# MoE 1 weights converted with an integer addition, a normalisation moved to ScalarE, and a second copy of values loaded by DMA

## The chip, the core and the metric

The kernel runs on one core of a Trainium2 chip. The metric is the device time in microseconds of one execution, the median of several. A core has TensorE (matrix products), VectorE, ScalarE and GpSimd (element-wise work), and SyncE, whose queue ("SP's queue" below) issues most DMAs here. Each engine works through its own instructions in order and waits on semaphores for the others.

## The reference

Three layers follow each other. Attention has 4 batches and 8 heads, 512 local and 32 global tokens, head size 64; a local token sees the 32 global ones and the local ones within 32 positions:

```python
s_ll = np.where(np.abs(pos[:, None] - pos[None, :]) <= 32, scale * q_l @ k_l.T, -1e9)
a_l = sm(np.concatenate([scale * q_l @ k_g.T, s_ll], axis=-1))
out_l = a_l @ np.concatenate([v_g, v_l], axis=2)
out_g = sm(scale * q_g @ k_all.T) @ v_all
```

Then MoE 1, a dense layer over all 2176 tokens (512 to 2048 to 512), whose two weight matrices are given in float64:

```python
h = x @ w_in
x = np.maximum(0.01 * h, h) @ w_out
```

Then MoE 2: each token goes to one of 8 experts, by the largest of its cosine products with the experts' embeddings, and its result is scaled by the gate:

```python
out[mask] = gate_w[mask, None] * (np.maximum(x[mask] @ w1[e], 0.0) @ w2[e])
```

## The kernel before

**Attention** works on 16 pairs of heads. A pair has four units (two row blocks of 128 times two heads). For unit `u`, `S(u)` computes two blocks of scores of 128x224 (192 local keys and 32 global ones), VectorE adds the mask and takes the maximum (L213), ScalarE takes the exponential with its sum (L218), VectorE the reciprocal of the sum (L222, L223). Then the two blocks are normalised, one on GpSimd and one on VectorE:

```python
        for i in range(2):
            eng = "pv"[i]
```

`TR(u)` transposes the probabilities two slots later, `AV(p)` multiplies them with the values four slots later. A window of 192 keys plus 32 global ones takes two products, and so the values lie in two arrangements: `ve`, in blocks of 128 rows shifted by 32, and `vb`, which holds the first 64 rows of each following block and the 32 global rows. `load_v(n)` fills `ve` by five DMAs and `vb` by two copies on ScalarE (L116, L117). Both have two buffers. `QK` transposes queries and keys, `GS`, `GT` and `GA` do the global tokens for every second pair.

**The conversion.** The weights of MoE 1 come as 64-bit words, in 32 pieces of 128x512. TensorE's products need them as a high and a low part whose sum is the float32 value. `conv_load(i)` loads piece i (two buffers, `raw`); `conv_abs(i)` takes on ScalarE the absolute value of the upper words (L357); `conv_bits(i)` puts the float32 word together on VectorE by five operations (L367, L368, L371, L374, L375); `conv_add(i)` adds the contribution of the low words on GpSimd (L384); `conv_split(i)` copies the high part on ScalarE (L390) and takes the difference on GpSimd (L391). One call of `conv()` does `conv_split(i - 1)`, `conv_bits(i)`, `conv_add(i)`, `conv_abs(i + 1)` and `conv_load(i + 2)`.

**The order.** TensorE's order is that of the program. On the other engines a planner with its own costs places the instructions, by priority, before the kernel runs. Slots 0 to 20 of attention run alone, with a `conv()` at every second one. Then steps of MoE 1 (`L1(i, f)`: 12 products into the hidden layer, then a copy on ScalarE (L691), the leaky maximum on VectorE (L692), a cast on ScalarE (L694) and a difference on VectorE (L695); `L2(i, f)`: 6 products out of it) alternate with attention slots, 0.65 slots per step, and each step for the first two row groups makes one call of `conv()` or more until the 32 pieces are done. Row groups 2 to 7 follow with the rest of attention. MoE 2 comes last and is not touched.

Of the kernel before, what the change touches and what calls it, by code (L numbers as in the profile page):

```python
# [8 lines left out]
F32 = mybir.dt.float32  # L9
F32R = mybir.dt.float32r  # L10
BF16 = mybir.dt.bfloat16
I32 = mybir.dt.int32
U32 = mybir.dt.uint32
I64 = mybir.dt.int64
AF = mybir.ActivationFunctionType
ALU = mybir.AluOpType
AX = mybir.AxisListType

P = 128
BIG = 3.0e38  # L20
NEG = -8.0e9
TINY = 1.125 * 2.0 ** -15
# [3 lines left out]
def kernel(  # L26
# [16 lines left out]
    nc = tc.nc  # L43
    B, H, SL, D = q_l.shape
    SG = q_g.shape[2]
    S_ = SL + SG
    NT, DM = out.shape
# [3 lines left out]
    NC = SL // P  # L51
# [12 lines left out]
    wide = w_in.dtype == I64  # L64
# [3 lines left out]
    sb = ctx.enter_context(tc.tile_pool(name="sb", bufs=1))  # L68
# [36 lines left out]
    def load_v(n):  # L105
        b, h0 = n // HP, 2 * (n % HP)
        hs = slice(h0, h0 + 2)
        ve, vb = ves[n % 2], vbs[n % 2]
        nc.sync.dma_start(ve[0:32, 0], v_g[b, hs].rearrange("h s d -> s h d"))
        nc.sync.dma_start(ve[32:P, 0], v_l[b, hs, 0:96].rearrange("h s d -> s h d"))  # L110
        for h in range(2):
            nc.sync.dma_start(
                ve[:, 1:NC, h, :], v_l[b, h0 + h, 96:96 + 3 * P].rearrange("(c p) d -> p c d", p=P)
            )
        nc.sync.dma_start(ve[0:32, NC], v_l[b, hs, 480:512].rearrange("h s d -> s h d"))
        nc.scalar.copy(vb[0:64], ve[0:64, 1:NC + 1])  # L116
        nc.scalar.copy(vb[64:96], ve[0:32, 0:1].to_broadcast([SG, NC, 2, D]))  # L117
        values[n] = ve, vb


# [6 lines left out]
        out=mask[:, :, 0:WIN], in_=mask[:, :, 0:WIN], pattern=[[0, 3], [1, WIN]],  # L127
# [3 lines left out]
        out=mask[:, :, 0:WIN], in_=mask[:, :, 0:WIN], pattern=[[0, 3], [-1, WIN]],  # L131
# [20 lines left out]
    def bank_of(name):  # L152
        return bank[name] if name in bank else "T"
# [39 lines left out]
    def S(u):  # L193
        n, c0, h = u // 4, 2 * ((u // 2) % 2), u % 2
        kT, _ = qkT[n]
        r = slice(D * h, D * h + D)
        sp = ps.tile([P, 2, WK], F32, tag=bank_of("sp"), name="sp")
        for i in range(2):
            c = c0 + i
            if n < NPAD:  # L200
                nc.tensor.matmul(sp[:, i, :], qz[:, h, c * P:(c + 1) * P], kT[:, c, :], start=True, stop=True)
            else:
                nc.tensor.matmul(  # L203
                    sp[:, i, :], qz[r, n % 2, c * P:(c + 1) * P], kT[r, c, :], start=True, stop=True,
                    tile_position=(D * h, 0),
                )
        pr = prs[u % NPR]
        nm = att.tile([P, 2], F32, tag="nm", bufs=4, name="nm")
        sm = att.tile([P, 2], F32, tag="sm", bufs=4, name="sm")
        for i in range(2):  # L210
            c = c0 + i
            m = 0 if c == 0 else (2 if c == NC - 1 else 1)
            nc.vector.tensor_tensor_reduce(  # L213
                out=pr[:, i, 0:WK], in0=sp[:, i, :], in1=mask[:, m, :], scale=-0.125, scalar=BIG,
                op0=ALU.add, op1=ALU.min, accum_out=nm[:, i:i + 1],
            )
        for i in range(2):
            nc.scalar.activation(  # L218
                out=pr[:, i, 0:WK], in_=pr[:, i, 0:WK], func=AF.Exp, bias=nm[:, i:i + 1], scale=-1.0,
                accum_out=sm[:, i:i + 1],  # L220
            )
        nc.vector.tensor_scalar(out=sm, in0=sm, scalar1=1e-9, scalar2=None, op0=ALU.add)  # L222
        nc.vector.reciprocal(out=sm, in_=sm)  # L223
        for i in range(2):
            eng = "pv"[i]
            if eng == "a":
                nc.scalar.activation(out=pr[:, i, 0:WK], in_=pr[:, i, 0:WK], func=AF.Copy, scale=sm[:, i:i + 1])
            else:
                (nc.gpsimd if eng == "p" else nc.vector).tensor_scalar(  # L229
                    out=pr[:, i, 0:WK], in0=pr[:, i, 0:WK], scalar1=sm[:, i:i + 1], scalar2=None, op0=ALU.mult  # L230
                )
        units[u] = pr
# [91 lines left out]
    NCV = 2 * KF  # L324
    raws, temps = {}, {}

    def conv_dst(i):
        f = i // 2
        if i % 2 == 0:
            fs = slice(f % KH * P, (f % KH + 1) * P)  # L330
            return wih[f // KH][:, :, fs], wil[f // KH][:, :, fs]
        return woh[f // KH][:, f % KH, :].unsqueeze(1), wol[f // KH][:, f % KH, :].unsqueeze(1)

    def conv_load(i):
        f = i // 2
        if i % 2 == 0:
            src = w_in[:, f * P:(f + 1) * P].rearrange("(k p) f -> p k f", p=P)
            shape = [P, KM, P]
        else:
            src = w_out[f * P:(f + 1) * P, :].unsqueeze(1)  # L340
            shape = [P, 1, DM]
        if wide:
            t = att.tile([P, 2 * DM], I32, tag="raw", bufs=2, name="raw")
            t = t.rearrange("p (k n) -> p k n", k=shape[1])
            nc.sync.dma_start(t, src.bitcast(I32))
            raws[i] = t.rearrange("p k (n t) -> p k n t", t=2)
        else:
            t = att.tile([P, DM], F32, tag="raw", bufs=2, name="raw")
            t = t.rearrange("p (k n) -> p k n", k=shape[1])
            nc.sync.dma_start(t, src)  # L350
            raws[i] = t

    def conv_abs(i):
        if wide and i in raws:
            t0 = sb.tile([P, DM], I32, tag="x2T", bufs=2, name="t0")
            t0 = temps[i] = t0.rearrange("p (k n) -> p k n", k=raws[i].shape[1])
            nc.scalar.activation(out=t0.bitcast(F32), in_=raws[i][:, :, :, 1].bitcast(F32), func=AF.Abs)  # L357

    def conv_bits(i):
        if not wide or i not in raws:  # L360
            return
        raw = raws.pop(i)
        low, top = raw[:, :, :, 0], raw[:, :, :, 1]
        t0 = temps[i]
        t2 = sb.tile([P, DM], I32, tag="x2", bufs=2, name="t2")
        t2 = t2.rearrange("p (k n) -> p k n", k=raw.shape[1])
        nc.vector.tensor_scalar(out=t0.bitcast(F32), in0=t0.bitcast(F32), scalar1=TINY, scalar2=None, op0=ALU.max)  # L367
        nc.vector.tensor_scalar(  # L368
            out=t0, in0=t0, scalar1=3, scalar2=0x3FFFFFF8, op0=ALU.logical_shift_left, op1=ALU.bitwise_and
        )  # L370
        nc.vector.scalar_tensor_tensor(  # L371
            out=t2, in0=top, scalar=-0x40000000, in1=t0, op0=ALU.bitwise_and, op1=ALU.bitwise_or
        )
        nc.vector.tensor_scalar(out=t0, in0=t2, scalar1=-0x800000, scalar2=None, op0=ALU.bitwise_and)  # L374
        nc.vector.scalar_tensor_tensor(  # L375
            out=t0.bitcast(F32), in0=low.bitcast(U32), scalar=2.0 ** -52, in1=t0.bitcast(F32),
            op0=ALU.mult, op1=ALU.mult,
        )
        temps[i] = t0, t2

    def conv_add(i):
        if 0 <= i < NCV and wide:
            t0, t2 = temps[i]
            nc.gpsimd.tensor_tensor(out=t2.bitcast(F32), in0=t2.bitcast(F32), in1=t0.bitcast(F32), op=ALU.add)  # L384

    def conv_split(i):
        if 0 <= i < NCV:
            hi, lo = conv_dst(i)
            src = temps.pop(i)[1].bitcast(F32) if wide else raws.pop(i)
            nc.scalar.copy(hi, src)  # L390
            nc.gpsimd.tensor_tensor(out=lo, in0=src, in1=hi.bitcast(F32), op=ALU.subtract)  # L391

# [2 lines left out]
    def conv():  # L395
        with tc.high_priority(offset=0):
            conv_()

    def conv_():
        i = cv[0]  # L400
        if i > NCV:
            return
        cv[0] += 1
        conv_split(i - 1)
        conv_bits(i)
        conv_add(i)
        conv_abs(i + 1)
        if i + 2 < NCV:
            conv_load(i + 2)

# [545 lines left out]
    for ve, vb in zip(ves, vbs):  # L956
        nc.vector.memset(ve[32:64, NC], 0.0)
        nc.vector.memset(vb[96:P], 0.0)
    load_v(0)
    load_qk(1)  # L960
    load_qk(2)
    load_v(1)
    for i in range(2):
        conv_load(i)
    conv_abs(0)

    NU = 4 * NHP
    LAG, AVL = 2, 4
# [88 lines left out]
    k = 0  # L1057
# [3 lines left out]
    while k < len(steps):  # L1061
        i, f = steps[k]
# [17 lines left out]
        while credit >= 0.5 and (hold or slot < bound):  # L1080
            if not hold:
                hold = att_parts(slot)
                slot += 1
                h = (len(hold) + 1) // 2
# [6 lines left out]
        n = (len(halves) + 1) // 2  # L1091
# [6 lines left out]
        if pend_r:  # L1098
            st, t = pend_r.pop(0)
# [125 lines left out]
```

## Time and profile before

| | |
|---|---|
| median of 3 runs | 965.67 us (965.29 to 968.04) |
| profiled execution, its time | 967.12 us |
| profiled execution, its span | 965.4 us |
| mean granted TensorE clock | 0.967 |
| TensorE products busy | 899.1 us, 93% of the span |
| VectorE busy | 696.4 us, 72% |
| ScalarE busy | 564.2 us, 58% |
| GpSimd busy | 280.2 us, 29% |

The span runs from the first to the last instruction of the core. The granted clock is that of TensorE: 1.00 is 2.4 GHz, 0.50 is 1.2 GHz, and a figure between is the mean of a stretch that has both. Busy shares over the whole span hide that stretches have different limits; they are read by stretch below. Products are pipelined, so TensorE's busy time is an upper bound of what it needs.

### The profile page before, as it was taken

The numbers are of one execution on the slowest core, as the hardware profiler recorded it, in microseconds if no ns is written. First come the engines' busy times: TensorE is split into PE (matmuls) and PEld (weight loads), VectorE is DVE, ScalarE is ACT, GpSimd is POOL, SyncE is SP. The second block draws the span as 40 slices with busy tenths as digits, with TensorE's granted clock in tenths as the row PEclk, the third lists the DMA queues.
The fourth block names the chain that finished last, engine by engine and source line by source line (L and its number), as shares of the span: only waits on it lengthen the run. The fifth ranks groups of instructions, "written<-read, shape, count | busy, mean of one in ns | idle before, by whom it ended". The sixth has DMA issues, their size and how long they took to land.

```text
span 965.4 us, 16184 instructions
## 1 busy us (share of the span) xinstructions
PE 899.1 (93%) x5578; PEld 747.9 (77%) x5578; DVE 696.4 (72%) x1722; ACT 564.2 (58%) x1206; POOL 280.2 (29%) x316
## 2 busy tenths in 40 slices
PE   7688877979999999999999999997799999999997
PEld 5565766768888888887888888986687888888885
DVE  7999999997554554544553534564988999999996
ACT  6777545465545554454452323256477888888885
POOL 4767656663121121121110100020223321222211
PEclk9987988989999999999999999999799999999999
DMA  6843333341011011010000000254613416919650
GB/s 163 186 121 110 111 108 102 91 132 24 23 39 43 23 38 42 1 39 20 2 12 13 12 12 12 60 170 186 51 48 119 134 44 221 359 33 381 210 201 25
DMA packets 92454, 89.82 MB, mean 93 GB/s; under 512 B 61191, under 2 KB 69511, under 8 KB 92370
## 3 DMA queue, kind: packets, MB, share of 16 engines
q1 hardware_dynamic: 88146, 77.99, 26.6%
q0 software_dynamic: 4224, 10.78, 4.0%
q8 instruction: 45, 0.74, 0.4%
q14 instruction: 39, 0.32, 0.1%
HBM read 137.14 MB, written 11.63 MB: 154 GB/s over the span
## 4 chain that ended last, share of the span: by engine, by line
PE 62%; issue 5%; DVE 5%; DMA 3%; ACT 1%; POOL 0%; SPq 0%; POOLq 0%; DVEq 0%
PE hps L684 16%; PE hp L910 9%; PE yp L938 8%; PE yp L706 6%; PE yp L708 5%; PE yp L707 5%; PE sp L203 3%; PE av L252 2%; PE pp L238 1%; PE tp L924 1%; DVE w2s L865 1%; DVE w1s L865 1%; DMA ids<-idl 1%; PE lp L514 1%; DMA out_dram<-yo,ids 1%
## 5 line engine op out<-in xcount | busy, mean ns | idle before, releaser
L692 DVE SCALAR_TENSOR_TENSOR gf<-gf 128x256 f32<-128x256 f32 (+1 forms) x144 | 62.9, 445 | 121.0 <-ACT gf L691 120.7
L910 PE MATMUL hp<-w1s,xgT 128*128 128x512 f32 x528 | 139.0, 413 | 0.0
L691 ACT COPY gf<-hps 128x256 f32<-128x256 f32 (+1 forms) x144 | 50.1, 359 | 145.8 <-PE hps L684 143.3
L938 PE MATMUL yp<-w2s,ht 128*128 128x512 f32 x528 | 130.8, 396 | 1.0 <-DVEq L1189 1.0
L938 PEld LDWEIGHTS yp<-w2s,ht 128*128 128x128 f32 x528 | 98.8, 188 | 25.7 <-DVEq L1189 1.4
L706 PE MATMUL yp<-woh,g 128*128 128x512 f32 x272 | 115.4, 424 | 1.8 <-ACT g L694 1.8
L910 PEld LDWEIGHTS hp<-w1s,xgT 128*128 128x128 f32 x528 | 100.0, 196 | 21.2
L708 PE MATMUL yp<-woh,g 128*128 128x512 f32 x272 | 108.9, 400 | 4.3 <-DVE g L695 4.3
L229 POOL TENSOR_SCALAR pr<-pr,sm 128x224 f32<-128x224 f32 x64 | 65.4, 1021 | 160.5 <-DVE sm L223 130.3
L707 PE MATMUL yp<-wol,g 128*128 128x512 f32 x272 | 108.3, 398 | 0.0
L694 ACT CAST g<-gf 128x256 fp32r<-128x256 f32 (+1 forms) x144 | 55.3, 394 | 71.5 <-DVE gf L692 71.5
L695 DVE TENSOR_TENSOR g<-gf,g 128x256 fp32r<-128x256 f32 (+1 forms) x144 | 66.2, 468 | 31.2 <-ACT g L694 25.9
L684 PE MATMUL hps<-xs,wih 128*128 128x256 f32 x448 | 77.6, 296 | 11.0 <-DVE nm L213 11.0
L684 PEld LDWEIGHTS hps<-xs,wih 128*128 128x128 f32 x448 | 66.8, 195 | 18.4 <-DVE nm L213 12.3
L684 PE MATMUL hps<-xl,wih 128*128 128x256 f32 x448 | 72.9, 285 | 0.0
L684 PE MATMUL hps<-xs,wil 128*128 128x256 f32 x448 | 72.6, 285 | 0.0
L946 POOL DMA_INDIRECT out_dram<-yo,ids x22 | 26.2, 1191 | 157.0 <-ACT yo L945 150.2
L218 ACT ACTIVATE pr<-pr,nm 128x224 f32<-128x224 f32 x128 | 60.8, 477 | 18.2 <-DVE nm L213 17.9
L708 PEld LDWEIGHTS yp<-woh,g 128*128 128x128 f32 x272 | 51.6, 190 | 19.3 <-DVE g L695 7.1
L684 PEld LDWEIGHTS hps<-xs,wil 128*128 128x128 f32 x448 | 62.6, 194 | 0.0
L684 PEld LDWEIGHTS hps<-xl,wih 128*128 128x128 f32 x448 | 62.6, 194 | 0.0
L706 PEld LDWEIGHTS yp<-woh,g 128*128 128x128 f32 x272 | 51.4, 189 | 14.0 <-issue 4.6
(267 smaller groups left out, 1933.7 us busy)
## 6 DMA issues: line engine op xcount, KB each, us to landing
w1a<-in_moe_w_dram SPq DMA_DIRECT2D x12, 2048.0 KB
w2a<-in_moe_w_dram SPq DMA_DIRECT2D x12, 2048.0 KB
w1b<-in_moe_w_dram SPq DMA_DIRECT2D x12, 2048.0 KB
w2b<-in_moe_w_dram SPq DMA_DIRECT2D x12, 2048.0 KB
raw<-in_moe_w_in_dram SPq DMA_DIRECT2D x16, 512.0 KB
raw<-in_moe_w_out_dram SPq DMA_DIRECT2D x16, 512.0 KB
x2d<-x SPq DMA_DIRECT2D x16, 256.5 KB
kn<-in_k_l_dram SPq DMA_DIRECT2D x32, 128.0 KB
```

The source lines that it names most:

```text
L218: nc.scalar.activation(out=pr[:, i, 0:WK], in_=pr[:, i, 0:WK], func=AF.Exp, bias=nm[:, i:i + 1], scale=-1.0, accum_out=sm[:, i:i + 1],)
L229: (nc.gpsimd if eng == "p" else nc.vector).tensor_scalar(out=pr[:, i, 0:WK], in0=pr[:, i, 0:WK], scalar1=sm[:, i:i + 1], scalar2=None, op0 ...
L684: nc.tensor.matmul(hps, ws[a][:, k], xs[c][k], start=(a + c + k == 0), stop=((a, c) == (1, 0) and k == KM - 1))
L691: nc.scalar.copy(gf, hps[:, cs])
L692: nc.vector.scalar_tensor_tensor(out=gf, in0=gf, scalar=0.01, in1=gf, op0=ALU.mult, op1=ALU.max)
L694: nc.scalar.copy(g[:, 0], gf)
L695: nc.vector.tensor_tensor(out=g[:, 1], in0=gf, in1=g[:, 0].bitcast(F32), op=ALU.subtract)
L706: nc.tensor.matmul(yp, g[:, 0], hi, start=(f == 0), stop=False)
L707: nc.tensor.matmul(yp, g[:, 0], lo, start=False, stop=False)
L708: nc.tensor.matmul(yp, g[:, 1], hi, start=False, stop=(f == KF - 1))
L910: nc.tensor.matmul(hp_, xT[:, a, k, :], w[:, c, k, :], start=(a + c + k == 0), stop=(c == 1 and k == KM - 1))
L938: nc.tensor.matmul(yp, ht[:, a, f, :], w[:, c, f, :], start=(j + a + c + f == 0), stop=(j == c == 1 and f == 3))
```

## The change

Three edits. First, `conv_round(i)` takes the place of `conv_abs(i)`: besides the absolute value it has ScalarE multiply the low words by 2^-29 and convert them to integers, into a second tile that takes the buffers (`x2`) in which the result lay before. `conv_bits(i)` then puts the truncated float32 word together in place, and a single addition of integers on VectorE adds the rounded low part, which replaces the masking L374, the product L375 and GpSimd's addition L384. The result now lies in the buffers tagged `x2T`. Second, the block that GpSimd normalised goes to ScalarE. Third, `vb` is no longer copied by ScalarE from `ve`, but loaded by five DMAs of its own; one more part of it is cleared at the start.

```diff
-        nc.scalar.copy(vb[0:64], ve[0:64, 1:NC + 1])
-        nc.scalar.copy(vb[64:96], ve[0:32, 0:1].to_broadcast([SG, NC, 2, D]))
+        for h in range(2):
+            part = v_l[b, h0 + h, 96:96 + 3 * P].rearrange("(c p) d -> p c d", p=P)
+            nc.sync.dma_start(vb[0:64, 0:NC - 1, h, :], part[0:64])
+            nc.sync.dma_start(vb[64:96, :, h, :], v_g[b, h0 + h].unsqueeze(1).to_broadcast([SG, NC, D]))
+        nc.sync.dma_start(vb[0:32, NC - 1], v_l[b, hs, 480:512].rearrange("h s d -> s h d"))
...
-            eng = "pv"[i]
+            eng = "av"[i]
...
-    def conv_abs(i):
+    def conv_round(i):
+
         if wide and i in raws:
-            t0 = sb.tile([P, DM], I32, tag="x2T", bufs=2, name="t0")
-            t0 = temps[i] = t0.rearrange("p (k n) -> p k n", k=raws[i].shape[1])
-            nc.scalar.activation(out=t0.bitcast(F32), in_=raws[i][:, :, :, 1].bitcast(F32), func=AF.Abs)
+            pair = []
+            for k in range(2):
+                t = sb.tile([P, DM], I32, tag=("x2T", "x2")[k], bufs=2, name=f"t{k}")
+                pair.append(t.rearrange("p (k n) -> p k n", k=raws[i].shape[1]))
+            temps[i] = pair
+            nc.scalar.activation(out=pair[0].bitcast(F32), in_=raws[i][:, :, :, 1].bitcast(F32), func=AF.Abs)
+            nc.scalar.activation(out=pair[1], in_=raws[i][:, :, :, 0].bitcast(U32), func=AF.Copy, scale=2.0 ** -29)
...
         nc.vector.scalar_tensor_tensor(
-            out=t2, in0=top, scalar=-0x40000000, in1=t0, op0=ALU.bitwise_and, op1=ALU.bitwise_or
+            out=t, in0=top, scalar=-0x40000000, in1=t, op0=ALU.bitwise_and, op1=ALU.bitwise_or
         )
-        nc.vector.tensor_scalar(out=t0, in0=t2, scalar1=-0x800000, scalar2=None, op0=ALU.bitwise_and)
-        nc.vector.scalar_tensor_tensor(
-            out=t0.bitcast(F32), in0=low.bitcast(U32), scalar=2.0 ** -52, in1=t0.bitcast(F32),
-            op0=ALU.mult, op1=ALU.mult,
-        )
-        temps[i] = t0, t2
-
-    def conv_add(i):
-        if 0 <= i < NCV and wide:
-            t0, t2 = temps[i]
-            nc.gpsimd.tensor_tensor(out=t2.bitcast(F32), in0=t2.bitcast(F32), in1=t0.bitcast(F32), op=ALU.add)
+        nc.vector.tensor_tensor(out=t, in0=t, in1=low, op=ALU.add)
+        temps[i] = t
...
         conv_split(i - 1)
         conv_bits(i)
-        conv_add(i)
-        conv_abs(i + 1)
+        conv_round(i + 1)
...
         nc.vector.memset(vb[96:P], 0.0)
+        nc.vector.memset(vb[32:64, NC - 1], 0.0)
```

## Rows read from the trace of the kernel before

**Rows 1.** Busy time of each engine by stretch, granted clock, DMA share, GB/s.

```profile
core 0: us, PE busy (x) PEld busy (x) DVE busy (x) ACT busy (x) POOL busy (x), PEclk, DMA share, GB/s
8.00:85.50 77.50, 63.44 (x492) 46.89 (x492) 72.09 (x252) 59.05 (x166) 48.48 (x56) 0.90 0.62 152
85.50:230.00 144.50, 119.58 (x792) 97.30 (x791) 141.14 (x302) 77.35 (x196) 90.90 (x77) 0.91 0.36 104
230.00:500.00 270.00, 267.61 (x1985) 227.16 (x1984) 136.23 (x568) 132.27 (x384) 49.04 (x70) 0.99 0.10 25
```

**Rows 2.** Groups of VectorE, 0 to 230 us: busy, mean ns, idle before.

```profile
L375 DVE SCALAR_TENSOR_TENSOR t<-raw,t 128x512 f32<-128x512 uint32 x32 | 29.1, 911 | 0.3
L371 DVE SCALAR_TENSOR_TENSOR t<-raw,t 128x512 int32<-128x512 int32 x32 | 26.7, 833 | 0.7
...
L367 DVE TENSOR_SCALAR t<-t 128x512 f32<-128x512 f32 x32 | 24.9, 778 | 0.9 <-ACT t L357 0.8
L374 DVE TENSOR_SCALAR t<-t 128x512 int32<-128x512 int32 x32 | 19.7, 614 | 0.0
L229 DVE TENSOR_SCALAR pr<-pr,sm 128x224 f32<-128x224 f32 x35 | 18.9, 541 | 0.1
L695 DVE TENSOR_TENSOR g<-gf,g 128x256 fp32r<-128x256 f32 x23 | 18.4, 800 | 0.5 <-ACT g L694 0.5
...
L692 DVE SCALAR_TENSOR_TENSOR gf<-gf 128x256 f32<-128x256 f32 x23 | 14.8, 645 | 0.0
```

**Rows 3.** Single lines, 0 to 230 us: count, then shortest, median, longest ns.

```profile
L371 DVE SCALAR_TENSOR_TENSOR t<-raw,t x32: 666/692/1786, 21.2 to 222.4; 128x512 int32<-128x512 int32 x32
...
L374 DVE TENSOR_SCALAR t<-t x32: 403/416/1515, 22.8 to 224.2; 128x512 int32<-128x512 int32 x32
```

**Rows 4.** Groups of VectorE, 230 to 500 us.

```profile
L695 DVE TENSOR_TENSOR g<-gf,g 128x256 fp32r<-128x256 f32 x60 | 25.3, 422 | 14.8 <-ACT g L694 14.2 <-PE yp L708 0.5
...
L229 DVE TENSOR_SCALAR pr<-pr,sm 128x224 f32<-128x224 f32 x29 | 10.0, 343 | 0.8
```

**Rows 5.** Timeline, 150 to 170 us: start us, duration us, instruction.

```profile
157.09 1.50 POOL L391 TENSOR_TENSOR wol<-t,woh 128x512 fp32r<-128x512 f32 x1
157.37 1.50 DVE L695 TENSOR_TENSOR g<-gf,g 128x256 fp32r<-128x256 f32 x1
```

**Rows 6.** Timeline, 435 to 452 us; in brackets the idle time before.

```profile
449.24 0.62 ACT L116 COPY vb<-ve 64x512 f32<-64x512 f32 x1 [6.51 <-issue]
...
451.07 0.50 PE L706 MATMUL yp<-woh,g 128*128 128x512 f32 x1 [1.80 <-ACT g L694]
```

**Rows 7.** Groups of VectorE, 8 to 85.5 us.

```profile
L374 DVE TENSOR_SCALAR t<-t 128x512 int32<-128x512 int32 x9 | 5.7, 631 | 0.0
```

**Rows 8.** Groups of GpSimd, 0 to 230 us.

```profile
L384 POOL TENSOR_TENSOR t<-t,t 128x512 f32<-128x512 f32 x32 | 44.7, 1396 | 23.2 <-DVE t L375 17.6 <-DVE sm L222 4.0 <-DVE gm L287 1.0
L229 POOL TENSOR_SCALAR pr<-pr,sm 128x224 f32<-128x224 f32 x35 | 38.9, 1112 | 30.9 <-DVE sm L223 27.1 <-DVE gm L284 1.6 <-PE kp L178 1.0
L391 POOL TENSOR_TENSOR wol<-t,woh 128x512 fp32r<-128x512 f32 x16 | 22.8, 1423 | 8.8 <-ACT woh L390 8.8
```

**Rows 9.** Groups of ScalarE, 0 to 230 us.

```profile
L218 ACT ACTIVATE pr<-pr,nm 128x224 f32<-128x224 f32 x72 | 34.3, 477 | 16.7 <-DVE nm L213 16.6
L357 ACT ACTIVATE t<-raw 128x512 f32<-128x512 f32 x32 | 21.7, 677 | 9.3 <-DMA raw<-in_moe_w_out_dram 5.4 <-DMA raw<-in_moe_w_in_dram 3.8
...
L694 ACT CAST g<-gf 128x256 fp32r<-128x256 f32 x23 | 9.4, 407 | 34.7 <-DVE gf L692 34.7
...
L117 ACT COPY vb<-ve 32x512 f32<-32x512 f32 x10 | 6.2, 617 | 1.1 <-DMA ve<-in_v_g_dram 0.6
```

**Rows 10.** Timeline, 0 to 30 us (SPq: DMA issues of SP's queue).

```profile
5.96 0.48 SPq L115 DMA_DIRECT2D ve<-in_v_l_dram  x1
...
8.09 0.62 ACT L116 COPY vb<-ve 64x512 f32<-64x512 f32 x1 [0.26 <-DMA ve<-in_v_l_dram]
...
14.32 0.43 SPq L345 DMA_DIRECT2D raw<-in_moe_w_in_dram  x1
```

**Rows 11.** Waits of SP's queue, whole run: total us, times, longest us.

```profile
SPq L112 <- PE av L252: 14.3, 6, 4.5
```

More of the change, by code (lines that the diff above doesn't have):

```diff
@@ L362, in conv_bits @@
         raw = raws.pop(i)
[L363 to L367, printed above, removed]
+        top = raw[:, :, :, 1]
+        t, low = temps[i]
+        nc.vector.tensor_scalar(out=t.bitcast(F32), in0=t.bitcast(F32), scalar1=TINY, scalar2=None, op0=ALU.max)
         nc.vector.tensor_scalar(
-            out=t0, in0=t0, scalar1=3, scalar2=0x3FFFFFF8, op0=ALU.logical_shift_left, op1=ALU.bitwise_and
+            out=t, in0=t, scalar1=3, scalar2=0x3FFFFFF8, op0=ALU.logical_shift_left, op1=ALU.bitwise_and
         )
         nc.vector.scalar_tensor_tensor(
-            out=t2, in0=top, scalar=-0x40000000, in1=t0, op0=ALU.bitwise_and, op1=ALU.bitwise_or
+            out=t, in0=top, scalar=-0x40000000, in1=t, op0=ALU.bitwise_and, op1=ALU.bitwise_or
         )
-        nc.vector.tensor_scalar(out=t0, in0=t2, scalar1=-0x800000, scalar2=None, op0=ALU.bitwise_and)
-        nc.vector.scalar_tensor_tensor(
-            out=t0.bitcast(F32), in0=low.bitcast(U32), scalar=2.0 ** -52, in1=t0.bitcast(F32),
-            op0=ALU.mult, op1=ALU.mult,
-        )
-        temps[i] = t0, t2
-    def conv_add(i):
-        if 0 <= i < NCV and wide:
-            t0, t2 = temps[i]
-            nc.gpsimd.tensor_tensor(out=t2.bitcast(F32), in0=t2.bitcast(F32), in1=t0.bitcast(F32), op=ALU.add)
+        nc.vector.tensor_tensor(out=t, in0=t, in1=low, op=ALU.add)
+        temps[i] = t
     def conv_split(i):
@@ L388, in conv_split @@
             hi, lo = conv_dst(i)
-            src = temps.pop(i)[1].bitcast(F32) if wide else raws.pop(i)
+            src = temps.pop(i).bitcast(F32) if wide else raws.pop(i)
             nc.scalar.copy(hi, src)
@@ L964 @@
         conv_load(i)
-    conv_abs(0)
+    conv_round(0)
     NU = 4 * NHP
```

## The prediction

> **What bounds the kernel now.** I read the profile in four steps. First the busy time by stretch [rows 1]. The kernel has an attention part (slots 0 to 20, 8 to 85.5 us), a mixed part where MoE 1 steps and attention slots alternate and the weight conversion runs (85.5 to 230 us), and a part where the conversion is over (from 230 us). In the mixed part VectorE is busy 141.14 of 144.50 us, 98%, TensorE 119.58 and ScalarE 77.35. In the attention part VectorE has 72.09 of 77.50 us (93%), TensorE 63.44, ScalarE 59.05. From 230 to 500 us TensorE has 267.61 of 270.00 and VectorE half. So VectorE sets the pace up to 230 us and TensorE behind it, and the order of TensorE's work is fixed in the program: time won before 230 us moves everything behind it forward.
>
> Second, what VectorE does there [rows 2]. The five operations of a conversion piece, 32 pieces, lead the list (one, L368, is not shown). Their means are odd: 614 ns for L374, whose median is 416 [rows 3]; 833 for L371, median 692; 800 and 645 for the MoE 1 lines L695 and L692, where L695 takes 422 after 230 us [rows 4]. L367 reads one tensor and writes one, of L374's size, so I take 416 for its unhindered price too, against a mean of 778.
>
> Third, why. The timeline shows it [rows 5]: GpSimd's subtraction begins at 157.09 and takes 1.50 us; VectorE's L695 begins at 157.37 and also takes 1.50, and so ends with it or just behind. VectorE is stretched by GpSimd's work.
>
> The stretch, (mean − unhindered) × count, from rows 2 to 4: L375 (911−692)×32 = 7.0 us; L371 (833−692)×32 = 4.5; L367 (778−416)×32 = 11.6; L374 (614−416)×32 = 6.3; L229 (541−343)×35 = 6.9; L695 (800−422)×23 = 8.7; L692 (645−422)×23 = 5.1. In all 50 us, 44 without L374.
>
> Fourth, behind 230 us: one place where ScalarE, in order, sat 6.51 us before the copy L116 into the second set of values; TensorE then stood 1.80 us [rows 6].
>
> **The change part by part.**
>
> *VectorE, conversion.* L374 goes: 19.7 us [rows 2], of which 5.7 in the attention part [rows 7] and 14.0 in the mixed one. L375 becomes an integer addition of two tensors, 128x512. The trace has no such addition. Bounds: 416 ns (one source, as L374 in [rows 3]) and 911 (L375 as it is now); the nearest row is L371, two sources of the same size, 692 unhindered. I take 692, so it is worth nothing against L375 beyond the stretch below. The ends move VectorE by ∓9 us over both parts.
>
> *GpSimd, and the stretch.* In the first 230 us the four kinds that read large tiles take 44.7 (L384) + 38.9 (L229) + 22.8 and about as much again (the two halves of L391; one is shown) = 129 us [rows 8]. The change removes L384 and GpSimd's L229; 45 remain, 35%. If the stretch falls in proportion, 0.65 × 44 = 28.4 us go: conversion 15.0, L229 4.5, L692 and L695 9.0. Ten of the 32 pieces and 20 of the 35 halves lie in the attention part, which gets 7.3; the mixed part gets 21.1. The ends are 0 and 44.
> The Trainium skill ("SBUF — State Buffer", section "Who interferes with whom") states that GpSimd and VectorE share a port pair by an exclusive lock, held for a whole instruction, that the loser blocks fully, and that a VectorE operation with two SBUF inputs contends with a GpSimd operation that reads. Rows 5 agree: 1.50 us beside 1.50. That rule speaks against my proportion, since what counts is whether a subtraction is still there to block one operation, and this is a rival below.
>
> *ScalarE.* The conversion gains a pass per piece, over the low words. No row has ScalarE reading an integer; bounds are 407 ns (L694, half the elements) and 1.4 us (GpSimd's price for that size), nearest the Abs pass L357 with the same strided source, 677 [rows 8, 9]. I take 677: 10 × 0.677 = 6.8 us in the attention part, 22 × 0.677 = 14.9 in the mixed one. At 1.4 us it would cost the attention part 7 us and the mixed one nothing. One normalisation per unit comes from GpSimd, 128x224 between SBUF tiles: between L694's 407 and L218's 477 ns, so 0.44: 20 × 0.44 = 8.8 and 15 × 0.44 = 6.6 us. The two copies of 617 ns per load of values go [rows 9] (one of the two is shown): five loads in each part, 6.2 us each.
>
> *Sums by part.* Attention: VectorE 72.1 − 5.7 − 7.3 = 59.1; ScalarE 59.05 + 6.8 + 8.8 − 6.2 = 68.5; TensorE at most 63.4. The busiest is now ScalarE. Mixed: VectorE 141.1 − 14.0 − 21.1 = 106.0; ScalarE 77.35 + 14.9 + 6.6 − 6.2 = 92.7. TensorE has 119.6 at a mean granted clock of 0.91 [rows 1]. Between the two levels, 1.2 and 2.4 GHz, that is 18% of 144.5 us, 26 us, at the lower one, which can have cost 13 us. So TensorE needs 107 to 120 us; I take 113, as the lower clock follows its waits and about half of those should go.
>
> *How full.* The busiest engine filled 93% and 98% of these parts. ScalarE at 93% makes the attention part 73.7 us, 3.8 less. In the mixed part TensorE and VectorE are now near each other and wait for each other in turn; I take 92%: 113 / 0.92 = 122.8 us, 21.7 less.
>
> *Queues.* Each load of values has five more DMAs on SP's queue. SP issues one in about 0.48 us at the start, one right behind the other, and the first weights are issued at 14.32 [rows 10]. Two loads of values lie ahead of them: 2 × 5 × 0.48 = 4.8 us later at most, 0 if the queue's order puts the new ones behind. I count 1 us, in the attention part. The second copy itself comes 2.4 us of issue later, then lands like the last old DMA, which was issued at 5.96 and used at 8.09; in place of 1.2 us of copies. That is covered: values are first used four slots, some 15 us, after their pair begins. The added memset of 32x128 at the start is one small operation per buffer before VectorE is busy.
>
> *Behind 230 us.* The copy that held ScalarE [rows 6] is gone, so the 1.8 us and a little clock: I count 2 us, between 0 and 5 (2.4 us in which TensorE idled and 1% of clock, both in [rows 1], at half speed 2.7). The 29 normalisations that ScalarE gets there, 13 us, lie beside TensorE at 99% and ScalarE at 132 of 270. MoE 2 is untouched.
>
> Sum: 3.8 − 1 + 21.7 + 2 = 26.5 us. The profiled execution has a span of 965.4 us and a time of 967.12; the median of the three timed runs is 965.67. The gain is taken from the median: 939 us.
>
> **The rivals.**
> *ScalarE waits in order.* The Abs of piece i+1 now writes the buffer that the GpSimd subtraction of piece i−1 still reads, and that subtraction starts only after ScalarE's own copy in the same call. If Abs is queued right behind that copy, ScalarE sits about one subtraction, 1.4 us [rows 8], per piece, and behind it stand the exponentials and the copies that TensorE waits for. Attention: 68.5 + 14 = 82.5, 5 more than before; mixed: 92.7 + 30.8 = 123.5, at 98% 126, 18.5 less; with 2 behind, 950. It speaks against it that other ScalarE work can be put between. From 0.9 us per piece the attention part gets longer than it was.
> *Whole blocks.* Every remaining subtraction still catches one operation, since it and the four conversion operations come from one call: no stretch is saved. Mixed: VectorE 141.1 − 14.0 = 127, at 95% 134, 10.6 less; attention 3; behind 2: 950. By the lock rule of the Trainium skill (“SBUF — State Buffer”, “Who interferes with whom”), taken strictly, it would go this way.
> *Full clock.* With VectorE out of the way TensorE stays at the upper level: mixed 107 / 0.97 = 110, attention 68.5 / 0.97 = 70.6: 34 + 7 + 2 = 43 less, 922. The clock of 0.99 behind 230 us speaks for it, the mixed part's chains through three engines against.
> *Slower: the weights starve.* Ten loads of values before 230 us put 2.4 us of issue and a wait for the buffer's last reader, up to 4.5 us [rows 11], ahead of weight loads in SP's queue; ScalarE already waits for weights, 9.3 us in all at L357 [rows 9]. All of it exposed is 69 us. It decides from 38%: at half, 939 + 34.5 = 973. Against it: the old loads carry the same waits, and weight buffers come free two operations earlier.
>
> **How the numbers follow.** Forecast 0.58; ScalarE's waits 0.12; whole blocks 0.08; full clock 0.11; starved weights 0.07; gain and queue cancelling within 0.3%, about what a measurement of this kernel can tell from no change, 0.04. So faster 0.89, same 0.04, slower 0.07. The forecast's own range, from the ends of the clock (107 to 120 us), of the addition and of the stretch, is 929 to 948; with the rivals on the fast side, 920 to 956.
>
> **What would show it.** Right: between 8 us and the end of the conversion VectorE's share falls from 96% to some 85% and TensorE's rises; L367, L371, L692 and L695 near 0.42 to 0.7 us; conversion over near 204 us, and from there the old pace; ScalarE near full in the attention part; no wait of ScalarE for values at some 425 us. Wrong: ScalarE waiting for GpSimd before Abs, or for weights; means of L695 still near 0.8; an addition or a low-word pass of over 1 us; a mixed part above 135 us.

## The result and the profile after

The change makes the kernel 0.9% faster: 958.65 us median of four runs against 965.91, ratio 0.9914 with an interval of 0.989 to 0.9938. 939 was forecast, 26.5 us less; it came to 7.3 us less, outside the range of 920 to 956. Two of the three stretches came out near the forecast, the third 21 us worse.

The marks are the first product of MoE 1 and the first product of its 27th step (twelve products into the hidden layer make a step; from there on the steps follow at the same pace in all versions until attention goes on). Busy time by stretch, changed kernel, columns as in [rows 1], the marks at 103.3 and 233.6 us:

```profile
8.00:103.30 95.30, 72.68 (x492) 53.99 (x492) 77.04 (x264) 73.73 (x200) 24.17 (x34) 0.77 0.65 168
103.30:233.60 130.30, 120.23 (x839) 100.51 (x838) 97.60 (x265) 86.02 (x221) 31.47 (x32) 0.95 0.35 97
233.60:500.00 266.40, 265.94 (x1999) 225.90 (x1998) 139.54 (x578) 139.65 (x407) 22.73 (x41) 1.00 0.12 30
```

The kernel before, from its first MoE 1 product to its 27th step (the attention part stands in [rows 1]):

```profile
85.50:237.60 152.10, 127.18 (x839) 104.08 (x838) 143.77 (x309) 80.08 (x203) 91.78 (x78) 0.92 0.34 99
```

The attention part took 95.3 us in place of 77.5, 17.8 more. The mixed part took 130.3 in place of 152.1, 21.8 less. From the 27th step to the end of the span it is 724.3 in place of 727.8, 3.5 less. Together 7.5 us. In the attention part no engine is near full. The granted clock fell from 0.90 to 0.77 there, and TensorE's 492 products of the part were busy 72.68 us in place of 63.44. How much of the 17.8 us the lower clock made by itself, and how much it only followed from TensorE's waits, no run separates.

VectorE's groups, changed kernel, 0 to 230 us (beside [rows 2]; L377, L374, L373, L232, L688, L691 are the old L371, L368, L367, L229, L692, L695, and L380 is the integer addition):

```profile
L377 DVE SCALAR_TENSOR_TENSOR t<-raw,t 128x512 int32<-128x512 int32 x32 | 25.8, 805 | 0.5
...
L380 DVE CUSTOM_DVE_ANT_0 t<-t,t 128x1024 uint16<-128x1024 uint16 x32 | 24.2, 755 | 0.2
L374 DVE TENSOR_SCALAR t<-t 128x512 int32<-128x512 int32 x32 | 20.0, 624 | 0.4
L373 DVE TENSOR_SCALAR t<-t 128x512 f32<-128x512 f32 x32 | 17.6, 549 | 7.6 <-ACT t L364 7.3
L232 DVE TENSOR_SCALAR pr<-pr,sm 128x224 f32<-128x224 f32 x36 | 17.3, 482 | 0.8
L688 DVE SCALAR_TENSOR_TENSOR gf<-gf 128x256 f32<-128x256 f32 x25 | 12.7, 507 | 17.8 <-ACT gf L687 17.8
L691 DVE TENSOR_TENSOR g<-gf,g 128x256 fp32r<-128x256 f32 x24 | 10.9, 455 | 2.2 <-ACT g L690 2.2
```

L691 has come from 800 to 455 ns and L688 from 645 to 507: GpSimd's stretch is mostly gone there. In the conversion it is not: L377 has 805 ns where it had 833, and L374 has 624 where its counterpart L368, not shown in [rows 2], had 545:

```profile
L368 DVE TENSOR_SCALAR t<-t 128x512 int32<-128x512 int32 x32 | 17.4, 545 | 0.2
```

The mean of the addition holds stretch too. Its shortest, median and longest ns, 0 to 230 us:

```profile
L380 DVE CUSTOM_DVE_ANT_0 t<-t,t x32: 669/690/1781, 30.6 to 183.7; 128x1024 uint16<-128x1024 uint16 x32
```

ScalarE's groups in the attention part of the changed kernel:

```profile
L365 ACT ACTIVATE t<-raw 128x512 int32<-128x512 uint32 x15 | 10.1, 671 | 3.5 <-DMA raw<-in_moe_w_in_dram 2.5 <-DMA raw<-in_moe_w_out_dram 1.0
L364 ACT ACTIVATE t<-raw 128x512 f32<-128x512 f32 x15 | 10.0, 669 | 7.6 <-DMA raw<-in_moe_w_out_dram 4.1 <-DMA raw<-in_moe_w_in_dram 3.1 <-POOL wil L388 0.3
L230 ACT ACTIVATE pr<-pr,sm 128x224 f32<-128x224 f32 x20 | 9.5, 484 | 0.1
...
L387 ACT CAST wih<-t 128x512 fp32r<-128x512 f32 x7 | 4.3, 621 | 0.3 <-DVE t L380 0.3
L387 ACT CAST woh<-t 128x512 fp32r<-128x512 f32 x7 | 4.3, 610 | 2.1 <-DVE t L380 2.1
```

and of the kernel before, 8 to 85.5 us, the line that answers to L387:

```profile
L390 ACT CAST wih<-t 128x512 fp32r<-128x512 f32 x4 | 2.5, 624 | 0.0
L390 ACT CAST woh<-t 128x512 fp32r<-128x512 f32 x4 | 2.5, 616 | 0.0
```

Fourteen conversion pieces have their high part before the first MoE 1 product, where eight had: on ScalarE six pieces of the mixed part now go ahead of attention work. The timeline of ScalarE shows what that does:

```profile
48.99 0.66 ACT L364 ACTIVATE t<-raw 128x512 f32<-128x512 f32 x1 [2.75 <-DMA raw<-in_moe_w_in_dram]
49.55 0.66 ACT L365 ACTIVATE t<-raw 128x512 int32<-128x512 uint32 x1
...
51.52 0.67 ACT L365 ACTIVATE t<-raw 128x512 int32<-128x512 uint32 x1
...
52.84 0.68 ACT L364 ACTIVATE t<-raw 128x512 f32<-128x512 f32 x1
...
54.33 0.49 ACT L230 ACTIVATE pr<-pr,sm 128x224 f32<-128x224 f32 x1
```

and that of TensorE, behind it:

```profile
54.87 1.11 PE L241 MATMUL pp<-ident,pr 128*128 128x128 f32 x4 [6.41 <-ACT pr L230]
```

ScalarE sat 2.75 us for a weight load, then did four weight passes and other work, and only then the normalisation for which TensorE had stood 6.41 us. The four transposes that follow take 1.11 us; early in the part, at 19.78 to 25.69 us, four of them took 0.66. SP's queue shows why the weights were late:

```profile
6.49 0.74 SPq L118 DMA_DIRECT2D vb<-in_v_l_dram  x1
7.28 0.59 SPq L119 DMA_DIRECT2D vb<-in_v_g_dram  x1
...
22.14 0.43 SPq L348 DMA_DIRECT2D raw<-in_moe_w_in_dram  x1
```

The first weights are issued at 22.14 us in place of 14.32 [rows 10], 7.8 us later, where 4.8 was my upper bound: the ten added DMAs hold the queue for 6.2 us, most of them 0.6 us each and not 0.48, and other loads went ahead too.

### The profile page after: what moved, and what is told of

Its sections match the earlier page's. It is cut to its first block, busy times and chain, and to the rows that moved or that the text cites. A ratio compares the mean times of both kernels' runs of the same rounds, so it can differ in the third digit from the quotient of the medians.

```text
span 957.9 us, 16074 instructions
## 1 busy us (share of the span) xinstructions
PE 900.4 (94%) x5578; PEld 750.6 (78%) x5578; DVE 656.5 (69%) x1692; ACT 591.0 (62%) x1270; POOL 169.2 (18%) x220
## 4 chain that ended last, share of the span: by engine, by line
PE 72%; DVE 9%; DMA 7%; issue 6%; ACT 4%; SPq 2%; POOL 1%; POOLq 0%; DVEq 0%; ACTq 0%
PE hps L680 19%; PE hp L906 9%; PE yp L934 8%; PE yp L702 7%; PE yp L704 6%; PE yp L703 6%; PE sp L206 4%; DMA raw<-in_moe_w_in_dram 3%; PE av L255 2%; PE pp L241 2%; PE tp L920 1%; DMA raw<-in_moe_w_out_dram 1%; DVE w2s L861 1%; DVE w1s L861 1%; DMA ids<-idl 1%
## 5 line engine op out<-in xcount | busy, mean ns | idle before, releaser
L688 DVE SCALAR_TENSOR_TENSOR gf<-gf 128x256 f32<-128x256 f32 (+1 forms) x144 | 59.9, 424 | 129.0 <-ACT gf L687 128.7
L691 DVE TENSOR_TENSOR g<-gf,g 128x256 fp32r<-128x256 f32 (+1 forms) x144 | 58.4, 414 | 32.6 <-ACT g L690 28.0
L861 DVE TENSOR_TENSOR w2s<-w2a,w2s 128x1024 fp32r<-128x1024 f32 x48 | 56.7, 1218 | 2.8 <-ACT w2s L860 2.6
L861 DVE TENSOR_TENSOR w1s<-w1a,w1s 128x1024 fp32r<-128x1024 f32 x48 | 56.6, 1218 | 1.7 <-ACT w1s L860 1.6
## 6 DMA issues: line engine op xcount, KB each, us to landing
kn<-in_k_l_dram SPq DMA_DIRECT2D x32, 128.0 KB
```

Of the source, the lines that this page charges most:

```text
L688: nc.vector.scalar_tensor_tensor(out=gf, in0=gf, scalar=0.01, in1=gf, op0=ALU.mult, op1=ALU.max)
L691: nc.vector.tensor_tensor(out=g[:, 1], in0=gf, in1=g[:, 0].bitcast(F32), op=ALU.subtract)
L861: nc.vector.tensor_tensor(out=w[:, 1, c], in0=src[:, c], in1=w[:, 0, c].bitcast(F32), op=ALU.subtract)
```

## The experiments

The edits: 1 is the conversion, 2 the normalisation on ScalarE, 3 the second values by DMA. There are four theories. **Q**: the added DMAs put off the weights in SP's queue. **S**: in the attention part each us of ScalarE's work shows, full or not. **P**, against S: only the normalisation's place in the chain of a unit costs. **T**, beyond S: VectorE's work counts as well. The versions were timed beside the kernel before, whose medians were 966.5 to 967.2 us.

| | edits | median, us | ratio, interval | first MoE 1 product | 27th step | pieces by the first product |
|---|---|---|---|---|---|---|
| before | none | 965.91 | | 85.5 | 237.6 | 8 |
| changed | 1, 2, 3 | 958.65 | 0.9914 (0.989 to 0.9938) | 103.3 | 233.6 | 14 |
| e1 | 2 | 970.79 | 1.0035 (1.0017 to 1.0054) | 94.8 | 241.7 | 11 |
| e2 | 3 | 970.38 | 1.0016 (0.9995 to 1.0038) | 87.5 | 244.7 | 8 |
| e3 | 1 | 949.94 | 0.9807 (0.9771 to 0.9843) | 87.2 | 221.2 | 11 |
| e4 | 1, 2 | 953.39 | 0.9848 (0.9806 to 0.9889) | 96.7 | 225.3 | 13 |
| e7 | 1, 3 | 943.88 | 0.9773 (0.9733 to 0.9813) | 83.3 | 217.1 | 9 |
| e9 | 2, 3 | 964.77 | 0.9972 (0.9946 to 0.9998) | 90.6 | 240.5 | 8 |

The first product and the 27th step are in us, read from the one profiled execution of each version. The last column counts the conversion pieces whose high part is made (`conv_split`) by the first product.

**Each edit alone, and the change without the third.**

> The kernel before with the second edit alone: GpSimd's normalisation goes to ScalarE. Theory Q (SP's queue: the five added DMAs per load of values put off the weight loads, and ScalarE, in order, waits for the weights): this run has no added DMAs, so the first MoE 1 product stays near 85.5 us (103.3 us in the changed kernel) and the mixed part gains from less GpSimd work, 950 to 960 us. Theory S (ScalarE has too much work in the attention part): 8.8 us more on ScalarE there, first MoE 1 product at 88 to 92 us, 958 to 968 us.

> The kernel before with the third edit alone: the second copy of values by DMA. Theory Q: weights 5 to 8 us later at the start and again at each load, first MoE 1 product at 90 to 103 us, 966 to 980 us. Theory S: ScalarE is relieved of two copies per load, first MoE 1 product at 83 to 86 us, 958 to 966 us.

> The kernel before with the first edit alone: the conversion by the low words on ScalarE and an integer addition. Theory Q: first MoE 1 product at 82 to 87 us, mixed part some 15 us shorter, 942 to 952 us. Theory S: 6.8 us more on ScalarE in the attention part with the copies kept, first MoE 1 product at 88 to 95 us, 950 to 960 us.

> The changed kernel without its third edit: values copied by ScalarE again. ScalarE has then the most work of all versions in the attention part. Theory Q: first MoE 1 product at 82 to 90 us, 935 to 948 us. Theory S: first MoE 1 product at 103 us or later, 958 to 970 us.

The edits are the three parts of the diff of the change, taken singly (e1 `"pv"` to `"av"`; e2 the loads of `vb` and its memset; e3 the conversion), and e4 is e1 with e3. The conversion alone is worth 17 us, more than the whole change. The normalisation alone puts the first MoE 1 product 9.3 us later, in the direction that S said but beyond its 88 to 92 us, and with the conversion again 9.5 (e3 to e4). The DMAs alone put it 2.0 us later, less than Q had it; the time is in Q's range. From e4 to the changed kernel they cost 6.6 us in the attention part and 5.3 in time. The attention parts of e2, e3 and e4, as busy time by stretch with the columns of [rows 1]:

```profile
8.00:87.50 79.50, 66.85 (x491) 50.20 (x492) 69.71 (x242) 51.16 (x150) 47.86 (x55) 0.85 0.64 162
8.00:87.20 79.20, 61.87 (x490) 46.88 (x491) 68.30 (x248) 65.90 (x178) 38.62 (x49) 0.94 0.67 168
8.00:96.70 88.70, 70.86 (x491) 52.14 (x492) 78.04 (x261) 78.70 (x210) 24.52 (x33) 0.83 0.65 162
```

These three speak against S as it stands. In e2 ScalarE has 7.9 us less work than before and the part is no shorter; its first weights are issued late, at 23.67 us, which can have taken the gain. In e3 it has 6.9 us more, with 3.8 less on VectorE, and the part is 1.7 us longer. e4 has the most work on ScalarE of all versions, but its part is 6.6 us shorter than the changed kernel's. S missed both its marks in all four runs, in e3 narrowly; Q missed both in e1 and e4 and has the time alone in e2 and e3. So neither holds throughout.

**A spare pass of ScalarE.** It reads a constant, and nobody reads what it writes. Each run has the first line and one of the others:

```diff
+        spare = att.tile([P, WK], mybir.dt.uint8, tag="spare", bufs=1, name="spare")
+        nc.scalar.activation(out=spare, in_=mask[:, 0, :], func=AF.Copy, scale=0.5)      # e5
+        nc.scalar.activation(out=spare, in_=mask[:, 0, :], func=AF.Copy, scale=nm[:, 0:1])  # e10, e13
+        nc.vector.tensor_scalar(out=spare, in0=mask[:, 0, :], scalar1=nm[:, 0:1], scalar2=None, op0=ALU.mult)  # e14
```

> The kernel before with one more pass of ScalarE per unit, 128x224, that reads a constant and whose result nobody reads: the second edit's work on ScalarE without its place in the chain of a unit. Moving the normalisation alone put the first MoE 1 product from 85.5 to 94.8 us. Theory S (ScalarE has too much work): the spare pass does the same, 92 to 95 us. Theory P (the probabilities of a unit now stand in ScalarE's queue behind other work, where GpSimd was free at once): 85 to 89 us. Time by S 968 to 976, by P 964 to 970 us.

> As the spare pass before, but scaled by the unit's own maximum, so that it can't run ahead of its unit: one pass of 0.39 us on ScalarE per unit that nobody waits for (the earlier one ran ahead, 43 passes and 16.5 us before 100 us). Theory S: first MoE 1 product 8 us later than 85.5, at 92 to 96 us, 969 to 974 us. Theory P (the place in the chain of a unit costs, not the work): 85 to 88 us, 965 to 968 us.

e5 took 986.02 us (1.0182, 1.014 to 1.0224), first product at 104.2: the passes were bound to nothing and 43 of them, 16.5 us, ran between 8 and 100 us. e10 took 974.07 (1.007, 1.0048 to 1.0092), first product at 94.3. The spare passes of e10 (number, then least, median and longest ns, first and last start in us):

```profile
L223 ACT ACTIVATE spare<-mask,nm x64: 464/467/486, 11.0 to 492.3; 128x224 uint8<-128x224 bf16 x64
```

and its attention part, as busy time by stretch:

```profile
8.00:94.30 86.30, 67.90 (x492) 50.72 (x492) 80.94 (x254) 66.72 (x185) 52.01 (x58) 0.86 0.61 148
```

Twenty passes of 0.467 us, 9.3 us, put the first product 8.8 us later, as much as the normalisation did in e1, though nothing needs what they write and ScalarE is busy 77%. So the place in the chain is not all that costs, against P, and added work on ScalarE shows, as S says. VectorE is busy 80.94 us here, 94% of the part and 8.9 us more than before, so this run alone does not tell ScalarE's queue from a slowed VectorE. Over both parts it is less: some 36 passes, 16.8 us, put the 27th step 8.1 us later, half a us per us.

**The same pass on the version with edits 1 and 3, on either engine.**

> First and third edits (943.9 us, first MoE 1 product at 83.3 us) and a spare pass of 0.47 us on ScalarE per unit, as in the paced run. Theory S (ScalarE alone sets the pace of the attention part) and theory T (ScalarE and VectorE take turns, and the work of both counts): first MoE 1 product 7 to 10 us later, at 90 to 94 us; 947 to 952 us. If ScalarE, busy 56.5 of 75.3 us here, has room: 83 to 86 us and 943 to 946 us.

> The same spare pass on VectorE, some 0.2 to 0.4 us per unit, 4 to 8 us in the attention part, where VectorE is busy 63.4 of 75.3 us. Theory S: first MoE 1 product stays at 83 to 85 us, 943 to 946 us. Theory T: it comes later by about the added work, 88 to 92 us, 946 to 952 us.

On ScalarE, 952.45 us (0.9839, 0.98 to 0.9879): 8.6 us more than e7, first product at 98.7, beyond the 90 to 94 expected, 27th step 9.6 later. On VectorE, at 0.33 us a pass (median; 0.41 in the mean over both parts), 947.42 (0.9797, 0.9762 to 0.9832): 3.5 more, first product at 87.9, 27th step 3.6 later. The attention part of e7 (busy time by stretch, columns as in [rows 1], here and below):

```profile
8.00:83.30 75.30, 61.75 (x491) 47.37 (x491) 63.43 (x236) 56.50 (x161) 38.29 (x48) 0.95 0.68 173
```

Of e13:

```profile
8.00:98.70 90.70, 67.89 (x491) 51.12 (x492) 74.71 (x257) 70.59 (x194) 41.30 (x52) 0.84 0.66 166
```

Of e14:

```profile
8.00:87.90 79.90, 65.51 (x491) 50.29 (x492) 71.52 (x267) 58.62 (x164) 38.34 (x50) 0.84 0.71 174
```

By this VectorE's work would cost a quarter of a us per us over both parts, but the intervals of e7 and e14 overlap, so T is not shown. In e13 ScalarE has 14 us more, of which 9.9 are the spare passes: twelve pieces lie before the first product, where e7 has nine. So conversion pieces also go ahead of attention when ScalarE has more work, and the mixed part, 128.0 us against 133.8, gives some of it back.

How much of the delay is added work, and how much is pieces that went ahead? It can be read earlier, where nearly as many pieces are done on either side: at the first exponential of the 14th unit, in the kernel before, e10, e7, e13 and e14:

```profile
53.31 0.50 ACT L218 ACTIVATE pr<-pr,nm 128x224 f32<-128x224 f32 x1
59.85 0.48 ACT L218 ACTIVATE pr<-pr,nm 128x224 f32<-128x224 f32 x1
58.64 0.48 ACT L221 ACTIVATE pr<-pr,nm 128x224 f32<-128x224 f32 x1
64.92 0.50 ACT L221 ACTIVATE pr<-pr,nm 128x224 f32<-128x224 f32 x1
56.74 0.51 ACT L221 ACTIVATE pr<-pr,nm 128x224 f32<-128x224 f32 x1
```

and busy time by stretch up to there, in the kernel before, e10 and e13:

```profile
8.00:53.30 45.30, 35.79 (x292) 27.11 (x292) 41.36 (x154) 35.66 (x104) 27.20 (x33) 1.00 0.74 176
8.00:59.90 51.90, 41.36 (x305) 31.33 (x307) 47.25 (x157) 41.88 (x121) 28.38 (x34) 0.93 0.67 153
8.00:64.90 56.90, 42.02 (x305) 32.79 (x307) 42.28 (x160) 42.61 (x121) 22.16 (x31) 0.85 0.69 165
```

In e10 the unit comes 6.5 us later, behind 13 spare passes of 6.1 us in all, with four high parts made and five pieces begun on VectorE on either side. At the 8th and the 11th unit it is the same: 3.1 and 4.7 us later, behind 3.3 and 4.7 us of passes, with as many pieces done. So in e10 the added work shows whole without pieces going ahead; but VectorE is 91% busy in both, and its work, 157 instructions against 154, took 5.9 us longer. In e13, where VectorE is busy 74%, the unit comes 6.3 us later than in e7, behind 13 passes of 6.2 us, with five high parts in both and three weight passes (2 us) more. Here single units scatter: 0.7 us at the 8th, 8.8 at the 11th. In e14, with 14 passes on VectorE ahead of it, the unit comes 1.9 us earlier than in e7. Up to this point, then, added work on ScalarE shows nearly whole and added work on VectorE does not. Of the 15.4 us by which e13 is late at the first product, 9.1 come behind the 14th unit, with eight more passes (3.7 us) and three pieces that went ahead.

**Both halves on VectorE, and the changed kernel without its second edit.**

> The first edit, and both halves normalised on VectorE; values copied by ScalarE. VectorE gets 0.34 us more per unit, 7 us in the attention part, to 75 of 79 us, and meets less GpSimd work. Theory P: VectorE comes to the half some 0.4 us after the other, so the first MoE 1 product stays near the 87 us of the first edit alone, and the mixed part is shorter as GpSimd stretches VectorE less: 943 to 949 us. Theory S says the same of ScalarE. If VectorE becomes the bound of the attention part, first MoE 1 product at 90 us or later, 949 to 956 us.

> The changed kernel without its second edit: GpSimd normalises again. Theory P: without the normalisation in ScalarE's queue first MoE 1 product at 88 to 94 us and 950 to 955 us. Theory Q (the added DMAs put off the weights): the late weights alone cost 6 us or more against the first edit alone (949.9 us), so 956 us or more.

e6 (`"vv"` on e3) took 953.65 us (0.988, 0.9835 to 0.9926), first product at 97.4, 27th step at 223.7: taking the normalisation from GpSimd costs the attention part the same 10 us on VectorE as on ScalarE. Neither P nor S foresaw that; the third forecast, VectorE as the bound, did. VectorE is busy 90% of the part:

```profile
8.00:97.40 89.40, 66.74 (x492) 50.78 (x492) 80.40 (x280) 70.65 (x187) 24.70 (x33) 0.84 0.64 161
```

So what the second edit costs is not a matter of ScalarE alone.

e7 was better than either theory had it, 943.88. From e7 to the changed kernel the second edit alone costs 14.8 us.

**The first weights ahead.**

```diff
+    for i in range(2):
+        conv_load(i)
     load_v(0)
     load_qk(1)
     load_qk(2)
     load_v(1)
-    for i in range(2):
-        conv_load(i)
```

> The changed kernel with the first two weight loads ahead of the first loads of values in SP's queue. Theory Q, first loads: what the DMAs added to the attention part (first MoE 1 product at 103.3 us, against 96.7 without them) is the first weights' place, 22.1 us for their issue: they now go before 12 us, first MoE 1 product at 96 to 99 us, 951 to 955 us. Theory Q, all loads: later weights are put off as before, at most 2 us won, 956 to 960 us.

> The first and third edits, GpSimd normalising as before, and the first two weight loads ahead of the first values in SP's queue. With ScalarE normalising, the place of the first weights was worth 6.6 us. Theory Q: it is worth as much here, 936 to 940 us against 943.9. Theory S: with less work on ScalarE late weights hide, 942 to 945 us.

On the changed kernel (e8), 952.08 us (0.9849, 0.9814 to 0.9885), 6.6 less, first product at 92.3, its part with a clock of 0.88:

```profile
8.00:92.30 84.30, 66.45 (x490) 48.99 (x491) 70.39 (x252) 69.36 (x190) 22.75 (x32) 0.88 0.70 170
```

Without the second edit (e11), 943.56 (0.9748, 0.9714 to 0.9782), the same as e7, though its first product is at 87.2; in e7 the first weights are issued at 24.23 us, later still than in the changed kernel. Of these four versions, late first weights cost only where ScalarE normalises too: Q holds with S, not alone.

**Edits 2 and 3 without the conversion.**

> The second and third edits on the kernel before, the conversion left as it was. Added up from each alone (+3.4 and +3.2 us against the runs beside them): about 973 us. Theory S (each us of work on ScalarE in the attention part shows): the copies that go pay for most of the normalisation that comes, first MoE 1 product at 88 to 92 us, 967 to 972 us. Theory Q (the weights that are issued late stop ScalarE in order, and the normalisation behind it): first MoE 1 product at 97 us or later, 974 us or more.

964.77 us, less than either alone; the first product, 90.6, is in the range of S, by which the copies that go pay for the normalisation; but neither the sum, nor Q, nor S foresaw that the time would be below that of the kernel before.

**The second values issued from GpSimd's queue** (`nc.gpsimd` in place of `nc.sync` for `vb`, with edit 1).

> The first and third edits with the second copy of values issued from GpSimd's queue, GpSimd normalising. Theory Q: SP's queue is as short as before the change, first weights issued near 14 us, 936 to 942 us. If writing the descriptors on GpSimd holds up its normalisation and subtraction, or VectorE, first MoE 1 product at 90 us or later and 946 to 955 us.

964.24 us (0.9968, 0.9953 to 0.9983), beyond both forecasts, first product at 105.3 with 14 pieces ahead of it, though the first weights were issued at 13.2 us. GpSimd's issues, 0 to 230 us:

```profile
L118 POOL DMA_DIRECT2D vb<-in_v_l_dram x20 | 13.3, 667 | 7.2 <-PE av L255 7.0 <-issue 0.2
L119 POOL DMA_DIRECT2D vb<-in_v_g_dram x20 | 11.6, 589 | 0.0
L120 POOL DMA_DIRECT2D vb<-in_v_l_dram x10 | 5.7, 566 | 0.0
```

31 us of GpSimd's time, with 7 us of waiting for the products that still read the buffer, stand in its order ahead of normalisations.

**The second edit only behind the attention part** (e7 with `("pv" if u < SLOT0 else "av")[i]`, and the same with `"vv"`).

> First and third edits, and the second one only from slot 21 on: GpSimd normalises in the attention part, ScalarE behind it. If the second edit's cost lies in the attention part alone: first MoE 1 product at 83 to 86 us, the mixed part 3 to 6 us shorter as GpSimd stretches VectorE less, 937 to 942 us. If it costs behind it as well: 945 us or more.

> As the run before, but from slot 21 on VectorE normalises both halves. VectorE gets 0.34 us more per unit there and loses GpSimd's stretch. First MoE 1 product at 83 to 86 us, 936 to 942 us if VectorE has room in the mixed part, 944 us or more if not.

947.16 us (0.9803, 0.9761 to 0.9845) and 944.1 (0.9755, 0.9713 to 0.9798). The mixed parts took 133.9 and 131.4 us, against 133.8 of e7: no gain worth the name. GpSimd's normalisation behind the attention part was not in the way.

## Why the prediction was wrong, and where it was right

**The step that failed** is "ScalarE at 93% makes the attention part 73.7 us", with the 1 us for SP's queue beside it. 2.8 us less was forecast, 17.8 more came. I took the part to be as long as its busiest engine's work by its share, so that ScalarE could take 9.4 us more, net, in the shade of the VectorE work that went. The spare passes show that added work finds no such shade: 9.3 us of work that nobody needs lengthened the part by 8.8, with ScalarE busy 77%, and at the 8th, 11th and 14th unit of e10 3.3, 4.7 and 6.1 us of it had cost 3.1, 4.7 and 6.5. Over both parts each us of added work on ScalarE costs half a us. That less work on ScalarE shortens the part is not shown: 7.9 us less did not (e2).

**The price of the second edit** is near what that gives. The spare pass has its length and count (0.467 against 0.484 us per unit) and cost 8.6 us on e7; the late first weights, once ScalarE normalises, 6.6 (e8). Together 15.2; from e7 to the changed kernel it is 14.8. That the two agree so closely is in part luck: at the first product the same sum is 15.4 + 11.0 = 26.4 us, against 20.0. GpSimd's normalisations, which I had counted as a gain through the stretch, give next to nothing behind the attention part once the addition L384 is gone (16 of the 36; e15, e16).

**The rivals.** That ScalarE would wait for GpSimd's subtraction ahead of Abs is refuted: 0.3 us in all before L364 in the attention part. "The weights starve" had the mechanism but not the size: the wait for weights in the attention part is 11 us (L364 and L365), against 3.5 at L357 before, and late first weights cost 6.6 us, not 34. "Full clock" did not come: 0.77 in the attention part, 0.95 in the mixed one. "Whole blocks" was nearly right for the conversion and wrong for MoE 1: by the working of the prediction L371, L367 and L368 (unhindered 692, 416 and 418) had 20.2 us of stretch and keep 14.5, while L695 and L692 had 13.8 and keep 2.9.

**What held.** The mixed part was to take 21.7 us less and took 21.8. That they agree so closely is luck, as six pieces of its conversion were done earlier; in e7, with one piece more than before ahead of it, it is 152.1 − 133.8 = 18.3. Behind, 2 was forecast and 3.5 came, and most of it comes with the values by DMA (e7 724.5 from the 27th step to the end, e3 728.5). The passes: 674 ns for the low words over the first 230 us against 677 taken, 484 for the normalisation against 440, 690 for the unhindered addition against 692. The stretch: (805−692)×32 + (549−416)×32 + (482−343)×36 + (507−422)×25 + (455−422)×24 = 15.8 us, against 44 − 28.4 = 15.6 left over in the forecast. Only the total agrees, as the rival above shows, and two terms are outside it: the addition, which has the place of L375 in the 44 and (755−690)×32 = 2.1 us of stretch, and L374, which I had left out and which was stretched more than before (624 ns, 545 as L368).

**What stays open.** The second edit costs 3 to 4 us alone or with the conversion, 15 with both others, and gains 5.6 with the third alone. Sums of single effects don't give these. The order on ScalarE and VectorE is made anew for each version, and the pieces ahead of the first product (8 to 14) go with it; how much of an effect is the new order and how much the work was not separated, as the order was not held fixed in any run; the reading at the 14th unit gets round it for the first part of the delay only. Why ScalarE's idle 23% cannot be used is shown at single places only (the wait for weights above).

## What to carry to other kernels

In a stretch where no engine is full, sizing a move by the busiest engine's share counts work as hidden that isn't: add a spare pass of the same length and measure what it costs before moving the work, and read the delay also at a mark up to which both versions have done the same work. Take a change of several edits apart: here the conversion with the values by DMA gives 943.9 us, and the edit in between took 15 of it back. An engine with time to spare and a slow operation (GpSimd, 1.11 us in [rows 8] against 0.48) can still be the right place for it, if the fast ones are those that attention passes through.

## What the runs showed of the hardware

The addition of 32-bit integers on VectorE runs as an operation on 128x1024 words of 16 bits and takes 690 ns in the median, as much as an unhindered operation with two sources of 128x512 (692 at L371); its mean of 755 is stretch. ScalarE's pass from unsigned to signed integers took as long as its pass over floats (674 and 668 ns with the same stride). Most of the added loads took 0.6 us each to issue on SP's queue (the last of each five 0.43); on GpSimd's queue they took 0.57 to 0.67 us of GpSimd itself.
